# Sliding-window attention and a gated conv FFN on one core: part of the conv in 32x32 tiles, with a new order of the work

## The chip, the cores and the metric

The kernel runs on one core of one Trainium2 chip. The metric is the device time of one execution in microseconds (us); the time before is the median of three runs, 217.72 us (216.22 to 221.8). A core has the engines TensorE (PE, with its weight loads as PEld), VectorE (DVE), ScalarE (ACT), GpSimd (POOL) and SyncE (SP, which issues DMAs here).

## The reference

Batch 8, 8 heads, 576 positions, head width 64; model width 512, hidden width 1024.

```python
scores = scale * np.matmul(q, k.transpose(0, 1, 3, 2))
mask = np.abs(pos[:, None] - pos[None, :]) <= 32
attn = softmax(np.where(mask, scores, -1e9))
x = np.matmul(attn, v).transpose(0, 2, 1, 3).reshape(B, S, 512)

h = np.maximum(x @ w_in, 0.0)
conv_out[:, s] = sum(conv_w[k] * h[:, s + k - 1] for k in range(3))   # per channel, zero outside
gate = 1.0 / (1.0 + np.exp(-conv_out))
out = (h * gate) @ w_out
```

## The kernel before

The program is one long list of steps, `ORDER`. Each word is a step's name with its arguments and, after `@`, the PSUM banks. A loop at the end of the kernel calls the steps in this order, and the class `Pinned` keeps every engine's instructions in program order; semaphores come from the dependences. So each engine, and the DMA queue of SyncE, is a queue in the order of the list, and what waits at its head holds up what is behind it. Nearly all instructions are issued through `Pinned`, which is why the profile shows them all under one line, L189; they are told apart by the tiles' names.

**Attention**, for batch b and half of the heads G: `lq`/`lk` load q and k (576 KB each), `cq`/`ck` cast them to bf16 (the last letter of a step tells the engine: a ScalarE, d VectorE, p GpSimd), `tq`/`tk` turn them on VectorE. `lv` loads a block of v, `cv` casts it into `ve`, `vo` makes a copy of `ve` that is shifted by 64 rows (two copies on an engine, or `t`, two DMAs). `sc` makes the scores of four or five tiles of 64 queries: 32 or 40 products of 32 rows by 128 columns, four at a time. The window's mask comes either from eight more matmuls on TensorE (`m`) or from `mk`, a product after the exponential `ex`. `av` multiplies by v, `nr` divides by the sum. The result is turned either by a DMA transpose (`xt`) or by TensorE (`xp`) and a copy (`xe`).

**FFN.** The 8 x 576 positions are cut into chunks of 384; the first two are halved. That makes 14 pieces P (four halves of 192, ten of 384). The hidden 1024 channels are eight blocks of 128, taken in four pairs m2, so there are 56 pairs. For each pair: `ph` (eight matmuls into PSUM), `re` (relu on ScalarE, into `hT`), `pc` (conv of three taps), `th` (tanh on ScalarE, since the gate is taken as 1 + tanh with the halves folded in), `ga` (gate on VectorE, into `gT`). Then `py` multiplies 128 rows by `w_out` (eight matmuls), `ye` copies from PSUM, `st` stores.

The conv is per channel, so as a matmul its weights are diagonal: `diag_w`, made by `dg`. `pc` has several kinds:

- P: whole 128x128 diagonals, three taps for each of the two blocks, six matmuls. Y: two taps on TensorE, the third by `tp`.
- A and D: 64x64 diagonals, twelve matmuls, of which four may run at once. The second block of the pair comes out with its two halves of 64 channels swapped. In A three tanh calls put that right, in D up to three gate calls. S swaps by DMA (`sw`).
- X: no matmul. ScalarE makes the first tap, VectorE's `tp` adds the other two by four `scalar_tensor_tensor` calls.

A `z` behind the kind says that the tanh goes to SBUF (`z`) and frees the PSUM bank. The heart of A and D is this:

```python
for kk in range(3):
    for i, m in enumerate(ms):
        for lo in (0, 64):
            to = 64 - lo if i else lo
            tensor.matmul(ps[to:to + 64, i, :], diag_w[lo:lo + 64, m, kk, lo:lo + 64],
                          taps(P, m, kk, lo), start=(kk == 0), stop=(kk == 2))
```

Weights: `li`/`ci` load and cast quarters of `w_in`, `lo`/`co` of `w_out`; they are staged in tiles that are not yet in use. `cw` turns the conv weights by one small matmul.

Of the kernel before, what the change touches and what calls it, by code (L numbers as in the profile page):

```python
# [31 lines left out]
lv,0,4 ck,0,0,p dg,3,a li,1 s7 cq,0,0,a dg,2,d li,2 ck,0,1,p dg,7,a tk,0,0 tq,0,0 li,0 cq,0,1,p tk,0,1 sc,0,0,0,m@0+2  # L32
li,3 cv,0,2,a sc,0,0,1,m@4+6 ex,0,0,0,0 lq,1,0 cv,0,0,p tq,0,1 ex,0,0,0,1 ex,0,0,1,1 lk,1,0 cv,0,1,d sc,0,1,0,m@0+2
ex,0,0,1,0 vo,0,0,d ex,0,1,0,1 sc,0,1,1,d@4+6 lq,1,1 cv,0,3,a dg,4,d av,0,0,0@2 lk,1,1 ex,0,1,1,1 cv,0,4,d nr,0,0,0
ex,0,1,1,0 ex,0,1,0,0 mk,0,1,1,d lv,1,2 ci,1,p vo,0,1,a av,0,1,0@0 nr,0,1,0 lv,1,1 ci,2,p xp,0,1@0 xp,0,0@1 xe,0,1,a
av,0,1,1@2 xe,0,0,d av,0,0,1@4 lv,1,0 ci,0,p nr,0,1,1 ph,0,2@0 ph,0,1@1 nr,0,0,1 re,0,2 lo,0 ci,3,p ph,0,0@2 re,0,1
pc,0,2,Pz@0 re,0,0 xp,0,3@1 lk,2,0 cq,1,0,p th,0,2,Pz pc,0,1,A@2 xp,0,2@4 xe,0,3,a ga,0,2,Pz ph,0,3@0 xe,0,2,a
pc,0,0,Pz@1 th,0,1,A lo,3 ck,1,0,p tq,1,0 ph,1,3@4 re,0,3 ga,0,1,A ph,1,0@5 th,0,0,Pz lq,2,0 cq,1,1,p tk,1,0 re,1,3
ph,1,2@6 re,1,0 xp,0,4@4 ga,0,0,Pz ph,1,1@5 re,1,2 lo,2 ck,1,1,p tq,1,1 xe,0,4,a sc,1,0,0,m@6+0 re,1,1 pc,1,2,P@4 lo,1
ex,1,0,0,1 cv,1,2,p tk,1,1 pc,0,3,P@5 ex,1,0,0,0 ph,2,3@0 th,1,2,P lk,2,1 cv,1,1,p th,0,3,P ga,1,2,P sc,1,1,0,d@6+2  # L40
lq,2,1 cv,1,0,a ph,2,2@1 ga,0,3,P ex,1,1,0,1 vo,1,0,d pc,1,3,Pz@4 re,2,3 ex,1,1,0,0 ph,2,1@5 lv,1,4 co,0,d re,2,2
av,1,0,0@6 th,1,3,Pz sc,1,1,1,m@0+2 mk,1,1,0,d re,2,1 pc,2,2,Pz@4 lv,1,3 ck,2,0,a ga,1,3,Pz nr,1,0,0 pc,1,1,Pz@5
th,2,2,Pz tk,2,0 th,1,1,Pz lq,3,0 co,3,p av,1,1,0@6 pc,2,3,P@4 ex,1,1,1,0 pc,1,0,P@5 ex,1,1,1,1 nr,1,1,0 ph,2,0@0
th,2,3,P lk,3,1 cq,2,0,p s6 th,1,0,P ga,1,1,Pz xp,1,0@6 xp,1,1@7 re,2,0 xe,1,0,a sc,1,0,1,m@0+2 lv,2,1 ga,2,3,P
xe,1,1,a pc,2,1,Y@6 ga,1,0,P co,2,a ph,3,3@4 ga,2,2,Pz lq,3,1 co,1,p tq,2,0 pc,2,0,Y@5 ex,1,0,1,1 ph,3,1@7 ex,1,0,1,0
tp,2,1,Y ph,3,2@2 re,3,3 lv,2,0 ck,2,1,p re,3,1 tp,2,0,Y py,0,2@4 th,2,1,Y re,3,2 ga,2,1,Y th,2,0,Y tk,2,1 lk,3,0
cq,2,1,p pc,3,3,Az@6 lk,4,0 pc,3,1,Dz@0 ye,0,2,a ga,2,0,Y cv,1,4,p py,0,1@2 th,3,1,Dz tq,2,1 th,3,3,Az lv,2,2 cv,1,3,p
ga,3,1,Dz vo,1,1,a sc,2,0,0,m@4+0 py,0,0@3 lv,2,3 cq,3,0,p ye,0,1,d ga,3,3,Az ex,2,0,0,1 lq,4,1 av,1,1,1@6 tq,3,0
ck,3,1,a py,1,0@2 st,0,1 cv,2,1,p nr,1,1,1 ex,2,0,0,0 ye,0,0,a av,1,0,1@0 tk,3,1 ye,1,0,a sc,2,0,1,d@4+6 st,0,0
cq,3,1,p ph,3,0@3 ex,2,0,1,0 nr,1,0,1 lv,2,4 pc,3,2,Pz@2 ex,2,0,1,1 re,3,0 sc,2,1,0,d@4+6 tq,3,1 th,3,2,Pz xp,1,2@0  # L50
st,1,0 ck,3,0,p xp,1,3@1 ex,2,1,0,0 xp,1,4@2 ex,2,1,0,1 pc,3,0,Pz@3 xe,1,3,d xe,1,2,a sc,2,1,1,m@4+6 mk,2,1,0,d
xe,1,4,a lk,4,1 tk,3,0 th,3,0,Pz ph,4,0@0 ex,2,1,1,1 lq,4,0 cv,2,2,p ga,3,2,Pz cv,2,0,a ex,2,1,1,0 ph,4,1@2 lv,3,0
ga,3,0,Pz ck,4,0,a mk,2,0,1,d py,1,2@4 re,4,0 tk,4,0 lv,3,2 cq,4,1,p re,4,1 lq,5,0 cv,2,3,a pc,4,0,A@0 tq,4,1 vo,2,0,t
ye,1,2,a ph,4,3@2 th,4,0,A cv,2,4,d lv,3,3 vo,2,1,d pc,4,1,P@4 lv,3,4 re,4,3 ga,4,0,A av,2,0,1@6 th,4,1,P pc,4,3,Az@2
st,0,2 ck,4,1,p nr,2,0,1 ph,4,2@0 th,4,3,Az ga,4,1,P lk,5,0 cq,4,0,p py,1,1@6 tk,4,1 re,4,2 lv,3,1 cv,3,0,p tq,4,0
pc,4,2,Pz@4 lk,5,1 cv,3,2,a ye,1,1,a ga,4,3,Az av,2,1,1@0 th,4,2,Pz sc,3,0,1,d@2+6 st,1,1 cq,5,0,p nr,2,1,1 ex,3,0,1,1
lv,4,0 av,2,1,0@4 ex,3,0,1,0 ga,4,2,Pz xp,2,4@0 xp,2,2@1 xe,2,4,a sc,3,1,1,m@2+6 xt,2,3 cv,3,3,p nr,2,1,0 py,2,0@0
ex,3,1,1,0 xe,2,2,d cv,3,4,a lv,4,2 mk,3,0,1,d ex,3,1,1,1 st,1,2 av,2,0,0@4 vo,3,1,d py,2,1@1 ye,2,0,a lv,4,3 ck,5,0,p
nr,2,0,0 lv,4,4 cv,3,1,a xp,2,0@0 ye,2,1,a xp,2,1@2 vo,3,0,d sc,3,0,0,d@4+6 xe,2,0,a py,2,2@3 xe,2,1,a tq,5,0 lk,6,1
ck,5,1,p ex,3,0,0,0 lk,6,0 ex,3,0,0,1 tk,5,0 sc,4,1,1,m@4+0 lv,4,1 cv,4,0,p ye,2,2,a av,3,1,1@6 mk,3,0,0,d lq,6,0  # L60
ph,5,0@2 ex,4,1,1,0 nr,3,1,1 ex,4,1,1,1 lq,5,1 cv,4,2,p av,3,0,1@4 re,5,0 st,2,1 sc,3,1,0,m@0+6 nr,3,0,1 pc,5,0,Pz@2
ex,3,1,0,0 lv,5,0 cv,4,3,p ex,3,1,0,1 tk,5,1 xt,3,2 cv,4,4,p sc,4,0,1,d@0+4 th,5,0,Pz ph,5,3@6 vo,4,1,d ex,4,0,1,0
# [24 lines left out]
ex,7,1,0,1 pc,10,3,Xz pc,10,2,Az@0 xt,6,0 py,7,0@2 mk,7,1,0,d th,10,0,Xz tp,10,3,Xz ye,6,0,a pc,10,1,Dz@4 th,10,2,Az
st,6,0 py,7,1@3 ye,7,0,d th,10,1,Dz ga,10,2,Az st,7,0 sc,7,0,0,d@6+0 th,10,3,Xz ph,11,3@4 ga,10,1,Dz ex,7,0,0,1
# [16 lines left out]
def kernel(  # L105
# [98 lines left out]
    def unit(b, G):  # L204
        return 2 * b + G
# [574 lines left out]
```

## Time and profile before

| what | value |
|---|---|
| median of 3 runs | 217.72 us |
| profiled execution | 217.15 us, of which the span 215.4 us |
| TensorE busy | 194.5 us (90%), 3113 matmuls |
| VectorE busy | 186.9 us (87%) |
| ScalarE busy | 181.4 us (84%) |
| GpSimd busy | 62.5 us (29%) |
| DMA | 47.58 MB, mean 221 GB/s; share of the 16 engines 75.4% |
| granted TensorE clock | 0.999 |

Busy time is the union of an engine's instructions, and the ends of matmuls are modelled. Rows of the profile read "line, engine, operation, out<-in, shapes, x count | busy us, mean ns of one | idle time before, and what ended it"; rows of a timeline read "start us, duration us, engine, line, operation". The span runs from the first to the last instruction.

### The profile page before, as it was taken

To read this page: it belongs to the slowest core of one execution; us is meant where nothing else is said; L and a number is where in the kernel's file an instruction comes from. 1 tells how busy PE (TensorE), PEld (TensorE's weight loads), DVE (VectorE), ACT (ScalarE), POOL (GpSimd) and SP (SyncE) were. 2 spreads that over 40 slices of the span, in tenths; PEclk is the share of its full clock that TensorE was granted. 3 is DMA by queue.
4 is the path that set the end of the run, shared out by engine and by line. 5 is a ranking of instruction groups with operands and counts; after the bars stand their busy time and mean duration, and the time that the engine had idled before them with its cause. 6 is when DMAs were issued, how large, how long until landed. Compare 5 with 4: busy or idle time off the path is not lost.

```text
span 215.4 us, 7416 instructions
## 1 busy us (share of the span) xinstructions
PE 194.5 (90%) x3113; PEld 116.0 (54%) x3134; DVE 186.9 (87%) x303; ACT 181.4 (84%) x318; POOL 62.5 (29%) x69
## 2 busy tenths in 40 slices
PE   2076998999999879999999999999999999999994
PEld 1055997855755546655445556455553554545443
DVE  5977499989999998998989898989899889999920
ACT  6686599899998767999977779999889898999951
POOL 5636754565323753340336050100300000000000
PEclk9999999999999999999999999999999999999999
DMA  6999999999999999999986569676236205311143
GB/s 222 315 245 394 382 287 401 332 326 337 315 375 264 324 193 348 288 242 306 262 284 186 128 158 246 138 194 185 102 94 109 97 27 158 95 34 49 53 190 146
DMA packets 63253, 47.58 MB, mean 221 GB/s; under 512 B 50012, under 2 KB 52596, under 8 KB 63220
## 3 DMA queue, kind: packets, MB, share of 16 engines
q1 hardware_dynamic: 63184, 47.10, 75.4%
q8 instruction: 24, 0.39, 0.8%
q14 instruction: 9, 0.07, 0.1%
q10 hardware_dynamic: 36, 0.01, 0.1%
HBM read 32.52 MB, written 9.44 MB: 195 GB/s over the span
## 4 chain that ended last, share of the span: by engine, by line
PE 63%; DVE 18%; ACT 5%; SPq 5%; issue 4%; DMA 4%; DVEq 0%
PE PS L189 63%; SPq L189 5%; DVE gT L189 3%; DVE qT L189 3%; DVE xn L189 3%; DVE kT L189 3%; DVE vo L189 3%; DMA vst<-in_v_dram 2%; DMA out_dram<-y 2%; ACT attn L189 2%; DVE attn L189 1%; ACT hT L189 1%; DVE rec L189 1%; ACT xT L189 1%; DVE xT L189 1%
## 5 line engine op out<-in xcount | busy, mean ns | idle before, releaser
L189 PE MATMUL PS<-xT,w_in_sb 128*128 128x385 bf16 (+3 forms) x448 | 70.9, 309 | 0.5 <-ACT z L189 0.4
L189 PE MATMUL PS<-w_out_sb,gT 128*128 128x512 bf16 (+1 forms) x275 | 65.5, 374 | 1.7 <-issue 0.9
L189 PEld LDWEIGHTS <-w_in_sb 128*128 128x128 bf16 x448 | 41.3, 100 | 22.4 <-issue 2.3
L189 DVE SCALAR_TENSOR_TENSOR gT<-z,hT 128x768 bf16<-128x768 f32 (+4 forms) x55 | 45.3, 838 | 5.2 <-ACT z L189 3.8
L189 ACT ACTIVATE hT<-PS 128x770 bf16<-128x770 f32 (+3 forms) x56 | 40.2, 731 | 6.8 <-PE PS L189 6.4
L189 PEld LDWEIGHTS <-gT 128*128 128x128 bf16 x296 | 26.9, 98 | 30.7 <-issue 2.8
L189 ACT ACTIVATE attn<-PS 128x512 bf16<-128x512 f32 (+1 forms) x64 | 39.0, 657 | 3.1 <-PE PS L189 2.7
L189 POOL TENSOR_SCALAR qb<-st 128x1152 bf16<-128x1152 f32 x25 | 32.2, 1288 | 30.7 <-DMA st<-in_q_dram 13.1
L189 ACT ACTIVATE z<-PS 64x384 f32<-64x384 f32 (+4 forms) x66 | 33.6, 512 | 4.4 <-PE PS L189 3.4
L189 DVE SCALAR_TENSOR_TENSOR z<-hT,conv_w_sb,z 128x384 f32<-128x384 bf16 x56 | 31.1, 618 | 0.6 <-ACT z L189 0.6
L189 PE MATMUL PS<-hT,diag_w 64*64 64x384 bf16 (+3 forms) x404 | 27.9, 307 | 0.0
L189 DVE TENSOR_TENSOR xn<-PS,rec 128x512 bf16<-128x512 f32 (+1 forms) x32 | 26.4, 824 | 1.1
L189 ACT COPY y<-PS 128x512 f32<-128x512 f32 (+1 forms) x30 | 17.3, 581 | 9.8 <-PE PS L189 8.9
L189 POOL TENSOR_SCALAR ve<-vst 128x512 bf16<-128x512 f32 x23 | 15.4, 676 | 33.3 <-DMA vst<-in_v_dram 26.0
L189 PE MATMUL PS<-qT,kT 32*128 32x64 bf16 x1152 | 15.7, 195 | 5.3 <-DVE qT L189 5.1
L189 DVE STREAM_TRANSPOSE qT<-qb 128x576 uint32<-128x576 uint32 x16 | 19.9, 1244 | 0.5 <-POOL qb L189 0.3
L189 DVE STREAM_TRANSPOSE kT<-qb 128x576 uint32<-128x576 uint32 x16 | 19.9, 1244 | 0.4 <-ACT qb L189 0.4
L189 PEld LDWEIGHTS <-diag_w 64*64 64x64 bf16 (+1 forms) x404 | 14.5, 104 | 10.4 <-issue 6.8
L189 PEld LDWEIGHTS <-kT 32*128 32x128 bf16 x1152 | 13.5, 96 | 10.8 <-issue 5.1
L189 PEld LDWEIGHTS <-attn 128*64 128x64 bf16 x640 | 13.3, 117 | 9.5 <-issue 6.3
L189 PE MATMUL PS<-ve,attn 128*64 128x65 bf16 x384 | 16.0, 203 | 2.4 <-ACT attn L189 1.4
L189 ACT ACTIVATE z<-hT,conv_w_sb 128x384 f32<-128x384 bf16 x28 | 15.7, 610 | 0.2
(53 smaller groups left out, 158.6 us busy)
## 6 DMA issues: line engine op xcount, KB each, us to landing
st<-in_k_dram SPq DMA_DIRECT2D x16, 576.0 KB, 6.3
st<-in_q_dram SPq DMA_DIRECT2D x16, 576.0 KB, 7.6
out_dram<-y SPq DMA_DIRECT2D x35, 256.0 KB, 2.8
vst<-in_v_dram SPq DMA_DIRECT2D x24, 256.0 KB, 6.1
vst<-in_v_dram SPq DMA_DIRECT2D x16, 192.0 KB, 5.8
vo<-ve SPq DMA_DIRECT2D x16, 130.0 KB, 2.4
xT<-in_moe_w_in_dram SPq DMA_DIRECT2D x2, 512.0 KB, 6.3
xT<-in_moe_w_out_dram SPq DMA_DIRECT2D x2, 512.0 KB, 7.0
```

The lines of the kernel that those rows point to most:

```text
L189: return lambda *args, **kwargs: tc.keep_in_program_order(do(*args, **kwargs))
```

## The change

1. **Conv of four blocks at once** (`pq`, kind Q) for six groups of two pairs, 12 of the 56: piece 5, 7 and 9 for blocks 4 to 7, piece 6, 8 and 11 for blocks 0 to 3. The diagonals are 32x32. Four row groups of four blocks are 16 tiles, each tap 16 matmuls, 48 in all. Block i comes out turned by 32 i channels; so that one tanh and one gate call serve a pair, the input of blocks 1 to 3 is turned beforehand: `rt` copies it by six DMAs into `hR`, and the weights of a Q group are turned likewise.
2. **Conv weights in three parts**: `cw` (matmul), `cwx` (copy to SBUF), and `cx0`, `cx`, `cxx` (a doubled copy, four turned matmuls, and a copy that picks the turned weights). `dg` now makes 64x64 diagonals, `dh` 32x32 ones. Kind P uses 64x64 diagonals too, twelve matmuls on two tiles. Small setup tiles live in two of the `y` tiles.
3. **Kinds S and Y go**, with `sw`.
4. **A new order**, for every engine. The counts of steps whose number changes:

| step | before | after |
|---|---|---|
| `pc` A (full, half) / D (full, half) / S | 16, 2 / 5, 1 / 2 | 7, 0 / 3, 0 / 0 |
| `pc` P (full, half) / Y half | 3, 11 / 2 | 2, 13 / 0 |
| `pc` X (full, half) | 14, 0 | 16, 3 |
| `pq` Q groups, `rt` | 0 | 6 (two pairs each) |
| `sc` with the mask on TensorE / `mk` d / `mk` p | 15 / 15 / 2 | 26 / 3 / 3 |
| `xt` / `xp` with `xe` (a, d) | 22 / 18 (14, 4) | 32 / 8 (7, 1) |
| `vo` DMA / VectorE / ScalarE | 8 / 6 / 2 | 3 / 12 / 1 |
| `cv` a / d / p | 10 / 7 / 23 | 11 / 2 / 27 |
| `cq`, `ck` a / d / p | 6 / 1 / 25 | 6 / 0 / 26 |
| `dg` a / d / p; `dh` d / p | 3 / 4 / 1; none | 1 / 0 / 7; 1 / 1 |

The diff, cut to its core (of the order only two lines with a Q group):

```diff
-lk,0,0 s5 s1 s3,d lq,0,0 s9 lk,0,1 s0,d lq,0,1 s4 lv,0,2 cw@0 lv,0,0 s2 s10 lv,0,1 dg,5,d dg,0,p lv,0,3 dg,6,d dg,1,a
+lq,0,0 s1 s2 s9 s0,d s4 s1d cw@2 lk,0,0 lk,0,1 lv,0,3 cq,0,0,p ck,0,0,a s10 cwx s7 dg,4,p tq,0,0 ck,0,1,p dg,5,a
...
+lv,7,3 ex,7,0,0,1 ex,7,0,0,0 ye,7,1,a ye,7,0,a pc,10,1,Az@0 av,7,0,0@2 av,7,1,0@4 ph,11,2@6 tp,10,0,Xz nr,7,0,0
...
+st,7,1 rt,11,0 xt,7,0 st,6,1 st,6,2 tp,11,2,Xz py,8,0@5 py,8,2@3 sc,7,0,1,d@6+0 py,8,1@2 ex,7,0,1,0 ex,7,0,1,1
+th,11,2,Xz pq,11,0,Qz@0+6 py,7,2@4 mk,7,1,1,d tp,11,3,Xz th,11,3,Xz th,11,1,Qz mk,7,0,1,d ga,11,3,Xz ga,11,2,Xz
...
+    hR_ = tiles(2, [128, 3, CH + 4], BF16, "hR")
-    diag_w = tiles(1, [128, MB, 3, 128], BF16, "diag_w")[0]
+    diag_w = [pp.tile([128, MB // 4, 4, 3, x], BF16, name=f"diag_w{x}") for x in (32, 64)]
...
+    def rt(P, q):
+        c, half = pieces[P]
+        kind = c % 3
+        n = CH + (4 if kind == 1 else 2)
+        h = hT_[kind].rearrange("p (q i) x -> p q i x", i=4)
+        for i in range(1, 4):
+            for p0, p1, a in ((0, 128 - 32 * i, 32 * i), (128 - 32 * i, 128, 0)):
+                sync.dma_start(hR_[q][p0:p1, i - 1, 0:n], h[a:a + p1 - p0, q, i, 0:n])
...
+    def tap(ps, P, m, kk, n, lo, to, h=None, i=0):
+        tensor.matmul(
+            ps[to:to + n], diag_w[n // 64][lo:lo + n, m // 4, m % 4, kk, :],
+            taps(P, m if h is None else i, kk, (lo, n), h), start=(kk == 0), stop=(kk == 2),
+        )
...
-        if kind[0] in "PY":
-            kks = (0, 1, 2) if kind[0] == "P" else (0, 2)
-            for i, m in enumerate(ms):
-                for kk in kks:
-                    tensor.matmul(
-                        ps[:, i, :], diag_w[:, m, kk, :], taps(P, m, kk),
-                        start=(kk == kks[0]), stop=(kk == kks[-1]),
-                    )
+        elif kind[0] == "P":
+            for i, m in enumerate(ms):
+                for kk in range(3):
+                    for lo in (0, 64):
+                        tap(ps[:, i, :], P, m, kk, 64, lo, lo)
...
+    def pq(P, q, kind, banks):
+        w = width(P)
+        for kk in range(3):
+            for i in range(4):
+                for r in range(4):
+                    tap(
+                        PS[:, banks[i // 2] + i % 2, 0:w], P, 4 * q + i, kk, 32, 32 * r, 32 * ((r + i) % 4),
+                        hR_[q] if i else None, i - 1,
+                    )
...
+    def cx(bank):
+        where["cx"] = PS[:, bank, 0:3 * MB]
+        for i in range(4):
+            tensor.matmul(
+                PS[:, bank, 3 * MB * i:3 * MB * i + 3 * MB], conv_w24[:, 32 * i:32 * i + 128], ident24,
+                start=True, stop=True,
+            )
...
+    def dh(q, e):
+        to = diag_w[0][:, q].rearrange("p i k x -> p (i k) x")
+        {"d": vector, "p": gpsimd}[e].tensor_tensor(
+            out=to, in0=eye32[:, None, :].broadcast_to([128, 12, 32]),
+            in1=conv_w_sb[0][:, q].rearrange("p i k -> p (i k)")[:, :, None].broadcast_to([128, 12, 32]),
+            op=ALU.mult,
+        )
```

More of the change, by code (lines that the diff above doesn't have):

```diff
@@ L36 @@
[L36 to L50, printed above, removed]
@@ L167 @@
     unit_ = band[:, 256:384].rearrange("p (e x) -> p e x", e=2)
-    band2 = tiles(1, [128, 192], BF16, "band2_")[0]
-    mask1 = tiles(1, [128, 64], BF16, "mask1_")[0]
-    conv_w24 = tiles(1, [3 * MB, 128], FP32, "conv_w24")[0]
+    once = y_[NY - 2]
+    mask1, eye32 = once[:, 0:32].bitcast(BF16), once[:, 32:48].bitcast(BF16)
+    eye64 = once[:, 128:160].bitcast(BF16)
+    conv_w_sb = [
+        t.rearrange("p (q i k) -> p q i k", i=4, k=3)
+        for t in (once[:, 48:48 + 3 * MB], tiles(1, [128, 3 * MB], FP32, "conv_w_sb")[0])
+    ]
+    conv_w24, ident24 = y_[NY - 1][0:3 * MB, 0:256], y_[NY - 1][0:3 * MB, 256:256 + 3 * MB]
     PS = pq.tile([128, 8, 512], FP32, name="PS")
@@ L207, in slot @@
     def slot(y, b, G):
[L208 to L211 removed]
+        return 4 * b + 2 * G + y
     def load_qk(y, b, G, *s_e):
[L216 to L224 removed]
         *s, e = s_e or ("s",)
@@ L241, in cast_qk @@
         cols = slice(s[0] * n, s[0] * n + n) if s else slice(0, 2 * n)
-        if b >= LATE:
-            cols = slice(0, 512 * len(blocks(G)))
         i = slot(y, b, G)
@@ L465, in re, with taps @@
         scalar.activation(to, ps, AF.Relu, bias=0.0, scale=0.5)
-    def taps(P, m, kk, part=None):
+    def taps(P, m, kk, part=None, h=None):
         c, half = pieces[P]
@@ L533, in pc, with tap_w @@
                     for lo in (0, 64):
-                        to = 64 - lo if i else lo
-                        tensor.matmul(
-                            ps[to:to + 64, i, :], diag_w[lo:lo + 64, m, kk, lo:lo + 64],
-                            taps(P, m, kk, lo), start=(kk == 0), stop=(kk == 2),
-                        )
+                        tap(ps[:, i, :], P, m, kk, 64, lo, 64 - lo if i else lo)
+    def pq(P, q, kind, banks):
+        w = width(P)
+        for kk in range(3):
[5 more added lines that the diff above has]
+                    )
+        for y in range(2):
+            m2 = 2 * q + y
+            where["pc", P, m2] = psum2(banks[y], w, True)
+            if kind[1:] == "z":
+                z_of(P, m2)
+    def tap_w(m, kk):
+        return conv_w_sb[1][:, m // 4, m % 4, kk:kk + 1]
     def tp(P, m2, kind):
-        ps = where["pc", P, m2]
-        for kk in ((1,) if kind[0] == "Y" else (1, 2)):
+        for kk in (1, 2):
             for i in range(2):
                 m = 2 * m2 + i
-                o = like(ps[:, i, :], P)
+                o = like(where["pc", P, m2][:, i, :], P)
                 vector.scalar_tensor_tensor(
-                    out=o, in0=taps(P, m, kk), scalar=conv_w_sb[:, kk, m:m + 1], in1=o,
-                    op0=ALU.mult, op1=ALU.add,
+                    out=o, in0=taps(P, m, kk), scalar=tap_w(m, kk), in1=o, op0=ALU.mult, op1=ALU.add
                 )
@@ L556, in tanh @@
             scalar.activation(out_, in_, AF.Tanh, bias=0.0, scale=1.0)
-        if kind[0] == "S":
-            tanh(where["z0s", P, m2], ps)
-            return
         if kind[0] != "A":
@@ L639, in cw @@
     def cw(bank):
-        tensor.matmul(PS[:, bank, 0:3 * MB], conv_w24, ident24, start=True, stop=True)
-        vector.tensor_copy(out=conv_w_sb.rearrange("p k m -> p (k m)"), in_=PS[:, bank, 0:3 * MB])
-    def dg(m, e):
-        if e != "a":
-            {"d": vector, "p": gpsimd}[e].tensor_tensor(
-                out=diag_w[:, m, :, :], in0=ident[:, None, :].broadcast_to([128, 3, 128]),
-                in1=conv_w_sb[:, :, m:m + 1].broadcast_to([128, 3, 128]), op=ALU.mult,
-            )
-        else:
-            for kk in range(3):
-                scalar.activation(
-                    diag_w[:, m, kk, :], ident, AF.Copy, bias=0.0, scale=conv_w_sb[:, kk, m:m + 1]
-                )
+        where["cw"] = ps = PS[:, bank, 0:3 * MB]
@@ new lines, in cw, with cwx, cx0 @@
+        tensor.matmul(ps, conv_w24[:, 0:128], ident24, start=True, stop=True)
+    def cwx():
+        vector.tensor_copy(
+            out=conv_w_sb[1].rearrange("p q i k -> p (q i) k"), in_=where["cw"].rearrange("p (k m) -> p m k", k=3)
+        )
+    def cx0():
+        vector.tensor_copy(out=conv_w24[:, 128:256], in_=conv_w24[:, 0:128])
+    def cx(bank):
[5 more added lines that the diff above has]
+            )
@@ new lines, in cxx @@
+    def cxx():
+        ps = where["cx"]
+        vector.tensor_copy(
+            out=conv_w_sb[0].rearrange("p q i k -> p i q k"),
+            in_=bass.AP(ps.tensor, ps.offset, [list(ps.ap[0]), [3 * MB + 1, 4], [4, MB // 4], [MB, 3]]),
+        )
+    def dg(m, e):
+        to, w = diag_w[1][:, m // 4, m % 4], conv_w_sb[1][:, m // 4, m % 4]
+        if e == "a":
+            for kk in range(3):
+                scalar.activation(to[:, kk, :], eye64, AF.Copy, bias=0.0, scale=w[:, kk:kk + 1])
+            return
+        {"d": vector, "p": gpsimd}[e].tensor_tensor(
+            out=to, in0=eye64[:, None, :].broadcast_to([128, 3, 64]),
+            in1=w[:, :, None].broadcast_to([128, 3, 64]), op=ALU.mult,
+        )
```

236 lines of the change are left out of this document (96 added, 140 removed).

## The prediction

> **What bounds the kernel now.** I read the page first (engine totals, then the 40 slices), then busy time by window, then TensorE's timeline, the groups by shape, and the tile view of `vo`.
>
> ```profile
> PE 194.5 (90%) x3113; PEld 116.0 (54%) x3134; DVE 186.9 (87%) x303; ACT 181.4 (84%) x318; POOL 62.5 (29%) x69
> ...
> PE   2076998999999879999999999999999999999994
> ...
> DVE  5977499989999998998989898989899889999920
> ACT  6686599899998767999977779999889898999951
> ...
> DMA  6999999999999999999986569676236205311143
> ```
>
> TensorE works in nine tenths or more of nearly every slice after the start, VectorE almost as much. The start is DMA: the queue is full, TensorE is not. The windows put numbers on that:
>
> ```profile
> 0.00:30.00 30.00, 17.51 (x358) 15.16 (x358) 22.30 (x52) 21.13 (x42) 18.64 (x27) 1.00 0.95 305
> 30.00:200.00 170.00, 164.60 (x2675) 94.78 (x2694) 158.62 (x244) 151.91 (x263) 43.89 (x42) 1.00 0.77 214
> 200.00:215.40 15.40, 12.42 (x83) 6.01 (x82) 6.00 (x10) 8.33 (x15) 0.00 (x0) 0.99 0.36 136
> ```
>
> Columns are length, then busy us of PE, PEld, DVE, ACT, POOL, then clock, DMA share, GB/s. From 30 to 200 us TensorE is busy 97%, VectorE 93%, ScalarE 89%. TensorE bounds, VectorE is four points behind, so a saving on TensorE alone is soon VectorE's time. The granted clock is 1.00 throughout and plays no part.
>
> Busy time overstates TensorE where matmuls overlap, so I price a step of the order from its first matmul to the next step's first:
>
> ```profile
> 130.21 0.40 PE L189 MATMUL PS<-band 32*128 32x256 bf16 x8
> 130.44 0.41 PE L189 MATMUL PS<-qT,kT 32*128 32x64 bf16 x32
> 130.78 1.48 PE L189 MATMUL PS<-xT,w_in_sb 128*128 128x385 bf16 x8
> ...
> 135.96 0.68 PE L189 MATMUL PS<-hT,diag_w 64*64 64x384 bf16 x12
> 136.57 1.90 PE L189 MATMUL PS<-w_out_sb,gT 128*128 128x512 bf16 x8
> 138.41 0.68 PE L189 MATMUL PS<-hT,diag_w 64*64 64x384 bf16 x12
> 139.02 0.42 PE L189 MATMUL PS<-qT,kT 32*128 32x64 bf16 x32
> ```
>
> A four-tile conv pair costs 0.61 us (136.57 - 135.96), the eight mask matmuls of a score step 0.23, its 32 products 0.34. In the same way: whole-array conv pair 1.07 (half piece 0.52), `ph` 1.34, `py` 1.83, `xp` 0.27. All steps together make 190.9 us. Of these 12.9 were begun by 30 us; the other 178.0 took the remaining 185.4, so 7.4 us are lost after the start, 2.9 of them the last copy and store.
>
> **The change, TensorE.** *Conv before:* 23 four-tile pairs x 0.615 + 3 halves x 0.35 + 3 whole-array x 1.07 + 11 halves x 0.52 + 2 two-tap halves x 0.34 = 24.8 us; the 14 X pairs cost TensorE nothing. *After:* 10 x 0.615 + 2 x 1.07 + 13 x 0.52 = 15.1 us, 19 X pairs, and six Q groups of two pairs, 48 matmuls of 32x32 each. No Q is in the trace. From below, three rounds in which sixteen tiles run at once: a whole-array stream is 1.07/6 = 0.179 us, so 0.54. From above, four tiles at a time: 12 x 0.179 = 2.15. The nearest row is the four-tile pair, whose three rounds take 0.615; issuing is no limit, since 40 score products go in 0.42 us (10.5 ns each; 48 make 0.50). I take 0.65, six make 3.9. Conv: 19.0 - 24.8 = -5.8.
>
> *Matmul floor, by a page:* the Trainium skill, "TensorE: Matmul & The Clock Gate", section "Wait — 56ns, not 53.3ns?", says matmul starts are never closer than about 25 ns. By it, as an estimate, a Q group would be 48 x 25 = 1.2 us and the six 3.3 us dearer. The 10.5 ns between score products here contradict it, so I leave it out.
>
> *Masks and transposes:* 26 instead of 15 score steps get the mask from TensorE (+11 x 0.25 = +2.7), and 8 instead of 18 blocks are turned by `xp` (-10 x 0.27 = -2.7). The `cx` matmuls fall in the start, where TensorE waits for inputs; without that cover they would cost some 0.6. Net: **-5.8**, leaving 185.1 besides `cx`, 185.7 with it.
>
> **VectorE and ScalarE.**
>
> ```profile
> L189 DVE SCALAR_TENSOR_TENSOR z<-hT,conv_w_sb,z 128x384 f32<-128x384 bf16 x56 | 31.1, 618 | 0.6 <-ACT z L189 0.6
> ...
> L189 ACT ACTIVATE z<-PS 64x384 f32<-64x384 f32 x32 | 15.5, 485 | 0.6
> ```
>
> ```profile
> L189 SPq DMA_DIRECT2D vo<-ve x16: 462/574/2524, 61.9 to 147.6; - x16
> L189 DVE COPY vo<-ve x12: 424/426/1385, 13.5 to 88.5; 64x1040 bf16<-64x1040 bf16 x12
> ```
>
> The figures after the first colon of the tile view are min/median/max ns. VectorE: `vo` 12 steps instead of 6, +8.1 at the mean of the old ones (two copies of 0.675); `tp` on 2 more full and 3 half pairs less 2 two-tap ones, +7.6; `mk` 3 for 15, -8.9; gates, one call of 0.95 where a crossed pair needs up to three, -3.1; `xe` -2.1; casts -2.1 (`cv`) and -1.1 (`ck`); `dg` -2.2 (to GpSimd, half as wide); small things +0.8. Sum -3.0, or -2.9 busy: 184.0. The soft number is `vo`: its copy takes 424 ns alone and up to 1385 while GpSimd works, so 24 copies cost 10 to 33 us; I take 16.2; GpSimd's extra 12 us of work (seven `dg`, one `dh`, four `cv`, a `mk`) could make it dearer.
>
> ScalarE: crossed four-tile tanh needs 0.497 + 2 x 0.485, a Q pair one call of 0.81; 18 crossed pairs become 7, -7.2. `xe` -3.5, `vo` -2.1, `dg` -2.0, X taps +4.5, `cv` +0.6: -9.7, some -8.9 busy. No bound.
>
> **Queues and start.** SyncE gains 36 copies for `rt` and 10 transposes and loses ten `vo` and four `z` copies. A `vo` copy is 0.574 us of issue, a transpose 1.25 (two in 2.52 us):
>
> ```profile
> 117.54 2.52 SPq L189 DMA_TRANSPOSE xT<-xn  x2
> 120.16 1.17 SPq L189 DMA_DIRECT2D vo<-ve  x2
> ```
>
> That is 20.9 + 12.5 - 8.3 = +25 us of SyncE time, most of it between `py` 2 and `py` 7. `pq` is a new wait: relu (0.8) -> six copies issued (3.5) -> landing (1.8, what `vo` shows after its issue) = 6.1 us. Hiding it is TensorE work between the last `ph` of the group and its `pq`: counted from the order, about 7.7 us at the tightest (piece 11), 8 to 12 elsewhere. Without cover the whole 6.1 is paid, with scores and `py` queued behind `pq`, and ScalarE's exp behind those. A transpose or two ahead in the queue (1.25 each) uses up the slack; I book 1.0 for all six.
>
> In the start two more loads of 576 KB stand ahead of the `w_in` quarters. GpSimd's `w_in` casts began at 17.36, 18.74, 20.07 and 21.45, 1.36 us per 512 KB, so the first quarter comes 3.1 us later, near 20.5, the last near 27.6. The first scores come earlier, one load being moved behind them. Stepping through the new order by hand to `sc 1 1 0` I get 13.0 us of TensorE steps by 30 us against 12.9. I count nothing (bounds -1 and +2).
>
> **Sum.** TensorE: 30 + (185.7 - 13.0) + 7.4 = 210.1. VectorE: 184.0, less 22.3 in the start and 1.1 of last copies, is 160.6; at 93% of the time, 172; so its last gate ends at 202.1. Half a us on, `py` 11 in four parts (5.5) and the 2.9 at the end give 211.0. I take 210.3 between the two and 1.0 for the `pq` waits: a span of 211.3. The profiled execution has 217.15 for a span of 215.4, so 1.75 outside: **213.0 us**. That execution lies 0.6 below the median 217.72, so against the median it is -2.2%, close to the 2% that a measurement of this kernel can just tell.
>
> **Rivals.**
>
> *A copy port that stays free* (209 or less). If the 12 `vo` steps meet an idle GpSimd, VectorE sheds 6 us more, is out of the way, and the loss after the start shrinks by 3: 215.4 - 5.8 - 3 + 1.75 = 208.4. For: half of the old copies took 424 to 427 ns. Against: GpSimd has 12 us more to do.
>
> *Q runs four tiles at a time* (222). Then +1.5 x 6 = 9. For: four row groups write one block, at different partitions of one bank. Against: the four-tile pair does that with two row groups, and 0.615 is far below the 6 x 0.179 = 1.07 of two at a time. The Trainium skill, "TensorEngine Tiling (Array Packing)", section "Restrictions and Gotchas", holds that different row tiles can't use one bank at once; by that rule Q would be this rival, and the trace speaks against it.
>
> *SyncE late* (224, slower). One mechanism: the `rt` copies stand behind transposes, loads and stores in one queue, and these wait for their own producers. If each of six groups reaches TensorE 2 us late, 12 us join the 211.9 of the bare TensorE line. It decides as soon as SyncE reaches `rt` more than 1.6 us after the relu in the tightest group. For: about 56 us of issue in a stretch with 63 of TensorE work. Against: the DMA share is down to a half by then, so copies land quickly.
>
> *The new order holds less well* (218). It is a wholly new order. At 94% after the start instead of 96, the gain is given back: 2% of 173 is 3.5, and 1.5 more from the start.
>
> **How the numbers follow.** Forecast 0.42, free port 0.16, four at a time 0.07, SyncE late 0.22, order 0.13. The forecast's own range is 210 to 216.5; the 2% line (213.4) cuts it, 0.29 below and 0.13 above. Faster: 0.29 + 0.16 = 0.45. Same: 0.13 + 0.05 of Q + 0.09 of the order = 0.27. Slower: 0.22 + 0.02 + 0.04 = 0.28. The range takes in the free port with Q at 0.54 (206.5) and SyncE late with a little over (225).
>
> **What would show it.** `hT`,`diag_w` groups of 32x32 with about 0.65 us to the next step (over 1 us: Q wrong); TensorE waits on DMA into `hR` under 2 us in all (over 8: SyncE late); VectorE near 184 busy with `vo` copies averaging 0.68; 13 us of TensorE steps by 30 us. A span above 215 with Q at 0.65 and no `hR` waits would make the sum wrong in its loss term, under 208 in its VectorE term.

## The result and the profile after

The changed kernel takes 225.03 us (median of 4 runs, 222.89 to 226.02), the kernel before, in the same comparison, 218.45 (216.22 to 221.8). The ratio is 1.037, 95% interval [1.030, 1.043]: slower, where 213.0 was forecast. The profiled execution of after is 224.56 us with a span of 222.8. Single runs of one kernel lie up to 5 us from its median. Some runs of a kernel, whatever it is, are slowed down by some per cent, so the ratios are taken from the other runs alone (the medians from all), and `a_noq_d` and `a_st_pool`, with only one of these in four, have none.

The totals and slices of the page of after:

```profile
PE 198.0 (89%) x3351; PEld 118.5 (53%) x3374; DVE 184.0 (83%) x299; ACT 171.3 (77%) x292; POOL 73.6 (33%) x91
...
PE   1478999896998988887999999989999999999994
...
DVE  4887988989569986981699989997999998899930
ACT  2895799875958936784778889689859988898941
...
PEclk9999999999999999996799999999999999999999
DMA  6999997997989999957999869986866554242043
```

VectorE and ScalarE have less to do than before (184.0 for 186.9, 171.3 for 181.4), and TensorE's 198.0 for 194.5 are partly at a lower clock. But slices 8 to 19 of TensorE have sixes, sevens and eights, VectorE and ScalarE have holes there, and in two slices the granted clock falls to 0.6 and 0.7. The windows (columns as in the prediction) say where the time went:

```profile
0.00:30.00 30.00, 20.29 (x429) 16.80 (x430) 23.91 (x50) 19.93 (x37) 23.26 (x43) 1.00 0.98 310
30.00:200.00 170.00, 158.09 (x2795) 91.87 (x2814) 146.43 (x228) 136.83 (x232) 50.36 (x49) 0.98 0.86 217
200.00:222.80 22.80, 19.59 (x132) 9.88 (x132) 13.67 (x23) 14.52 (x25) 0.00 (x0) 1.00 0.31 116
```

Between 30 and 200 us TensorE is busy 93% instead of 97%, VectorE 86% instead of 93%. No engine's work became the bound; all wait more. I priced TensorE's steps as in the prediction and took the sum of the steps begun by a time from that time. The loss is 16.2 us at 30 us (before 17.1), 23.1 at 90 (20.6), 30.1 at 110 (20.1), 33.4 at 150 (21.1), and then stays. So about ten of the twelve lost us go between 90 and 150 us.

The first Q group stands there. TensorE's timeline (in brackets the idle time before an entry and what ended it):

```profile
95.68 2.98 PE L195 MATMUL PS<-xT,w_in_sb 128*128 128x386 bf16 x17
99.39 0.34 PE L195 MATMUL PS<-hT,diag_w 32*32 32x384 bf16 x4 [0.74 <-ACT hT L195]
99.79 0.73 PE L195 MATMUL PS<-hR,diag_w 32*32 32x384 bf16 x6
100.78 0.34 PE L195 MATMUL PS<-hR,diag_w 32*32 32x384 bf16 x2 [0.26 <-DMA hR<-hT]
101.29 0.32 PE L195 MATMUL PS<-hR,diag_w 32*32 32x384 bf16 x1 [0.18 <-DMA hR<-hT]
102.10 0.50 PE L195 MATMUL PS<-hR,diag_w 32*32 32x384 bf16 x3 [0.49 <-DMA hR<-hT]
...
103.17 0.61 PE L195 MATMUL PS<-band 32*128 32x256 bf16 x8
103.57 0.64 PE L195 MATMUL PS<-qT,kT 32*128 32x64 bf16 x32
```

The group comes in drops, one copy into `hR` after the other, and takes 103.17 - 99.39 = 3.78 us. The piece 8 group takes 2.55. The others take 0.74 to 0.97, so Q itself is not far from the 0.65 that was forecast. After it the same score step that took 0.42 us takes 0.64. The windows of 2 us around this place show why:

```profile
100.00:102.00 2.00, 1.17 (x9) 0.30 (x6) 0.00 (x0) 0.05 (x1) 0.94 (x1) 0.91 0.38 81
102.00:104.00 2.00, 1.90 (x75) 1.20 (x74) 0.10 (x1) 0.81 (x1) 0.00 (x0) 0.50 0.83 244
104.00:106.00 2.00, 1.30 (x49) 1.02 (x41) 0.97 (x2) 1.74 (x3) 0.00 (x0) 0.50 1.06 241
106.00:108.00 2.00, 2.00 (x45) 1.16 (x38) 1.95 (x3) 1.26 (x4) 0.60 (x1) 0.50 1.03 396
108.00:110.00 2.00, 2.00 (x47) 1.28 (x46) 0.46 (x2) 1.82 (x3) 1.62 (x2) 0.89 1.08 332
```

The clock stands at 0.50 from about 101.6 to 108.4 us: 3.4 us of TensorE time at most. VectorE and ScalarE do next to nothing from 100 to 104, as what they work on comes from TensorE.

And the queue of SyncE ahead of that group, where relu (`re`) had ended at 90.38:

```profile
87.23 3.79 SPq L195 DMA_TRANSPOSE xT<-xn  x1
91.08 0.57 SPq L195 DMA_DIRECT2D out_dram<-y  x1
91.75 3.41 SPq L195 DMA_TRANSPOSE xT<-xn  x2
95.25 0.52 SPq L195 DMA_DIRECT2D st<-in_k_dram  x1
95.88 4.15 SPq L195 DMA_DIRECT2D hR<-hT  x5
```

SyncE reaches `rt` at 95.88, 5.5 us after the relu. In the other groups it is 5.3, 4.6, 2.8, 0.5 and 0.4 us late. Adding up the queue's rows from 90 to 150 us, SyncE spends 52.2 of 60 us issuing (before 44.9) and has gaps of over 0.2 us for 3.1 us in all (before 11.5): in that stretch it has hardly any room.

### The profile page after: what moved, and what is told of

Read it like the earlier page. It is cut to its first block, busy times and chain, and to the rows that moved or that the text cites. A ratio compares the mean times of both kernels' runs of the same rounds, so it can differ in the third digit from the quotient of the medians.

```text
span 222.8 us, 7903 instructions
## 1 busy us (share of the span) xinstructions
PE 198.0 (89%) x3351; PEld 118.5 (53%) x3374; DVE 184.0 (83%) x299; ACT 171.3 (77%) x292; POOL 73.6 (33%) x91
## 4 chain that ended last, share of the span: by engine, by line
PE 60%; DMA 17%; SPq 7%; ACT 5%; DVE 4%; issue 3%; POOL 2%; POOLq 0%; DVEq 0%; ACTq 0%
PE PS L195 60%; DMA st<-in_k_dram 7%; SPq L195 7%; DMA xT<-xn 3%; DMA hR<-hT 3%; ACT attn L195 2%; DMA vst<-in_v_dram 2%; DMA out_dram<-y 2%; POOL attn L195 1%; DVE kT L195 1%; ACT z L195 1%; POOL qb L195 1%; DVE xn L195 1%; DVE y L195 1%; ACT y L195 1%
## 5 line engine op out<-in xcount | busy, mean ns | idle before, releaser
L195 PE MATMUL PS<-w_out_sb,gT 128*128 128x512 bf16 (+1 forms) x273 | 64.5, 373 | 1.9 <-issue 1.0
L195 DVE SCALAR_TENSOR_TENSOR gT<-z,hT 128x768 bf16<-128x768 f32 (+2 forms) x56 | 46.0, 846 | 9.5 <-ACT z L195 8.9
L195 ACT ACTIVATE hT<-PS 128x770 bf16<-128x770 f32 (+3 forms) x56 | 39.6, 728 | 9.6 <-PE PS L195 9.1
L195 DVE SCALAR_TENSOR_TENSOR z<-hT,conv_w_sb,z 128x384 f32<-128x384 bf16 (+1 forms) x76 | 42.5, 626 | 0.2
L195 ACT ACTIVATE z<-PS 128x768 f32<-128x768 f32 (+2 forms) x43 | 26.1, 621 | 7.0 <-PE PS L195 6.7
L195 POOL TENSOR_SCALAR ve<-vst 128x512 bf16<-128x512 f32 x27 | 18.7, 704 | 22.9 <-DMA vst<-in_v_dram 22.8
L195 PE MATMUL PS<-hT,diag_w 64*64 64x192 bf16 (+2 forms) x372 | 21.8, 297 | 0.8 <-ACT hT L195 0.7
L195 ACT ACTIVATE z<-hT,conv_w_sb 128x384 f32<-128x384 bf16 (+1 forms) x38 | 20.3, 591 | 0.2
L195 PE MATMUL PS<-band 32*128 32x256 bf16 (+1 forms) x208 | 14.0, 309 | 5.7 <-ACT band L195 4.2
L195 PEld LDWEIGHTS <-kT 32*128 32x128 bf16 x1152 | 15.3, 97 | 6.0 <-issue 4.3
```

The costliest lines, as they stand in the source:

```text
L195: return lambda *args, **kwargs: tc.keep_in_program_order(do(*args, **kwargs))
```

## The experiments

Each ratio is to the kernel before, run beside it on the same chip, with its 95% interval. Kernels named `a_` start from after, `b_` from before.

**Is it the order, the Q groups, the queue's loads, or TensorE's transposes?**

`b_order`: the new code with the old order.

```diff
-ORDER: after's
+ORDER: before's, its two S pairs as A, its two Y halves as P; no rt, no pq
```

> The changed program with the old order: the conv weights are made the new way (64x64 diagonals, cw and cwx), no Q group, two S pairs made A, two Y halves made P. If the loss lies in the new order of work (theory O), this runs like before: 217 to 220 us. If the new way of the weights and the P kind on two tiles cost something by themselves, 222 or more.

Measured 222.18 us, 1.018 [1.006, 1.029]. So even the old order loses some 2% with the new code.

`a_noq`: the six groups as two A pairs each.

```diff
-rt,5,1  ...  pq,5,1,Qz@0+4  th,5,2,Qz  ga,5,2,Qz
+             pc,5,2,Az@0 pc,5,3,Az@4  th,5,2,Az  ga,5,2,Az
```

> The changed kernel with the six Q groups undone: each is two A pairs at the same place, and the 36 rt copies are gone. Theory Q (the rt copies and the waits of pq hold the kernel up): pq took 6.3 us over its price in the trace, two A pairs cost TensorE 0.4 us more each; with SyncE 21 us freer 217 to 220 us. Theory S (early transposes in SyncE's queue hold the loads up, between 40 and 110 us): only the waits at 99, 146 us go, 221 to 224 us. Theory O: 223 to 226.

Measured 225.19 (221.35 to 227.48), 1.024 [1.008, 1.039]. Without Q and its copies nothing is won. By its ranges that spoke for theory O, but it could not tell: the A pairs that take Q's place cost about as much as the copies (see `a_nort` and `a_noq_d`).

`a_xp12`: seven of the DMA transposes go back to TensorE.

```diff
-xt,1,3
+xp,1,3@4 xe,1,3,a        (and 1,4 1,2 2,0 2,1 2,2 2,4)
```

> The changed kernel with the seven DMA transposes of batches 1 and 2 made by TensorE again (xp and xe on ScalarE, at the same place of the order). Theory S: DMA no longer runs dry at 49 to 56 and 64 to 66 us, the loss between 30 and 110 us falls from 13.9 by half or more; TensorE pays 1.9: 217 to 221 us. Theory Q: 224 to 227 us (the price of xp on top).

Measured 229.94, 1.049 [1.033, 1.066]. Theory S fell, and the time is over the range of theory Q too: 9 us off SyncE's queue in the early part bought nothing.

`a_loads`: within each cluster of SyncE's steps, `rt` first, then loads, then transposes and stores.

```diff
-xt,2,0 xt,2,1 ... lv,4,0 lv,4,2
+lv,4,0 lv,4,2 lq,5,0 lk,5,0 xt,2,0 xt,2,1
```

> The changed kernel with the order of SyncE's queue alone changed: within each run of DMA steps that stand together in the order, the rt copies come first, then the loads, then transposes, stores and vo. Theory S: 219 to 222 us, since loads no longer wait behind transposes that wait for xn. Theory Q: 222 to 224 by the earlier rt alone. Theory O: no change, 224 to 226.

Measured 240.4, 1.105 [1.095, 1.114], over all three ranges. The loads had not been what was late for TensorE; the stores and transposes put behind them are. The waits of this kernel (engine, line, what it waited for, us in all, times, longest) show it:

```profile
ACT y L195 <- DMA out_dram<-y: 23.7, 6, 7.9
...
PE PS L195 <- ACT y L195: 12.2, 4, 6.4
...
PE PS L195 <- DMA xT<-xn: 4.3, 2, 3.9
```

A tile `y` is free for the next `ye` only when its store has landed. ScalarE waits for that in its `ye`, and TensorE waits for ScalarE; this is more than what TensorE waits for the transposes themselves.

**Is it the copies?**

`a_nort`: no copies; `hR` is set to zero once, so three of four blocks in a Q group see zeros.

```diff
-rt,5,1   (and the five others)
+        for t in hR_:
+            gpsimd.memset(t, 0.0)
```

> The changed kernel with the rt copies left out; the turned input of the Q groups is zeros written once, so three of four blocks of a group get no conv. TensorE's 48 matmuls a group stay. Theory SyncE late (SyncE reached rt 5.5, 5.3, 4.6, 2.8, 0.5 and 0.4 us after the relu, and pq waited): the waits go and SyncE has 21 us less to issue, 216 to 219 us. Theory DMA traffic (transposes and loads are late by themselves): 222 to 224.

Measured 215.05 (213.57 to 218.17), 0.992 [0.975, 1.009]. Its profile:

```profile
30.00:200.00 170.00, 163.30 (x2890) 95.82 (x2902) 154.91 (x247) 147.14 (x248) 51.91 (x52) 1.00 0.84 212
200.00:212.10 12.10, 8.69 (x47) 4.51 (x48) 2.94 (x5) 4.19 (x9) 0.00 (x0) 1.00 0.40 152
```

TensorE is back at 96%, the clock at 1.00, and the span is 212.1 where the forecast had 211.3. With Q's matmuls kept, leaving the copies out takes away the whole loss against before, as far as the interval can tell.

**Can they stand elsewhere?** `a_rt_act` issues them from ScalarE's queue, `a_rt_pool` from GpSimd's, `a_rt_early` leaves them with SyncE but right behind the group's second relu.

```diff
-                sync.dma_start(hR_[q][p0:p1, i - 1, 0:n], h[a:a + p1 - p0, q, i, 0:n])
+                scalar.dma_start(hR_[q][p0:p1, i - 1, 0:n], h[a:a + p1 - p0, q, i, 0:n])
```

> The changed kernel with the 36 rt copies issued from ScalarE's queue, behind the relu that makes their input, instead of SyncE's. Theory SyncE late: the copies start at once, 219 to 222 us, the rest of the gain being lost to some 20 us of issue on ScalarE, which was busy 171 of 223. If what costs is the copies' landing, no change: 223 to 226.

> The changed kernel with the rt copies issued from GpSimd's queue, which was busy 74 us of 223. Theory wait: the copies start when the relu ends unless a cast or a load's wait stands ahead of them in GpSimd's queue; 217 to 222. Theory issue: SyncE is rid of 21 us, 216 to 220. If GpSimd's own waits for loads hold the copies up: over 225.

> The changed kernel with each rt moved forward in SyncE's queue to right behind the second relu of its group, ahead of the transposes, stores and loads that stood before it. Theory SyncE late by its order: pq no longer waits, 220 to 223 us. Theory SyncE late by its sum (it has too much to issue between 85 and 150 us, whatever the order): the transposes come later instead, 224 to 229.

ScalarE: 243.51, 1.122 [1.103, 1.141]. GpSimd: 224.74, 1.024 [1.014, 1.034]. SyncE early: 231.25, 1.060 [1.038, 1.082]. On ScalarE's timeline:

```profile
91.98 8.54 ACTq L195 DMA_DIRECT2D hR<-hT  x6
100.57 0.70 ACT L195 ACTIVATE attn<-PS 128x640 bf16<-128x640 f32 x1 [10.95 <-DMA hR<-hT]
```

Six issues there keep ScalarE from its exp and relu for 8.5 us, and TensorE stands still behind it. On GpSimd the copies wait for the relu with casts behind them (the tile view of `hR` has its idle time ahead of them and what ended it):

```profile
L195 POOL DMA_DIRECT2D hR<-hT x36: 501/517/740, 89.1 to 184.3; - x36
its engine sat idle before it (us, times) until:
  ACT hT L195: 22.3, 6
```

Early on SyncE, `rt` is issued within 1 us of the relu, and the time is worse: now the transposes and stores come later. The longest wait of TensorE, from 127 to 134 us, is again for a `ye`, which waits for a store:

```profile
133.38 0.59 ACT L195 COPY y<-PS 128x512 f32<-128x512 f32 x1 [7.47 <-DMA out_dram<-y]
...
134.01 3.26 PE L195 MATMUL PS<-w_out_sb,gT 128*128 128x512 bf16 x8 [6.75 <-ACT y L195]
```

In none of the three other places are the copies free.

**The waits or the issuing?** `a_rt_nowait` issues all 36 copies, but the Q groups read `hT` unturned and wait for none.

```diff
-                        hR_[q] if i else None, i - 1,
+                        None, i - 1,
```

> The changed kernel with all 36 rt copies issued, but pq reads hT as it stands instead of the turned hR, so three of four blocks of a group get other channels' input. SyncE has the same to issue, TensorE no longer waits for a copy. Theory wait (what costs is pq, first in TensorE's queue, waiting for the landing): 215 to 218 us, as without the copies (215.05). Theory issue (21 us of issue hold up the transposes, loads and stores behind them): 221 to 225.

Measured 222.5, 1.017 [1.012, 1.022]. Against 1.037 the waits are worth 2.0% (4.3 us); against 0.992, 36 copies that nobody waits for still cost 2.5% (5.5 us). With intervals of 1 to 2% on both differences, neither part can be called the larger. A piece of the second part is the wait seen above: TensorE waits 3.0 us for a `ye` (in `a_rt_one` 0.3).

```profile
ACT y L195 <- DMA out_dram<-y: 9.9, 4, 5.2
...
PE PS L195 <- ACT y L195: 3.0, 3, 1.9
```

`a_rt_one` makes one unturned copy of a group's six; `a_rt_tiny` makes all six, but of 16 columns each. The first edit is that of `a_rt_tiny`; the line of the second stands in `a_rt_one` in place of `rt`'s two loops.

```diff
-                sync.dma_start(hR_[q][p0:p1, i - 1, 0:n], h[a:a + p1 - p0, q, i, 0:n])
+                sync.dma_start(hR_[q][p0:p1, i - 1, 0:16], h[a:a + p1 - p0, q, i, 0:16])
```
```diff
+        sync.dma_start(hR_[q][:, :, 0:n], h[:, q, 1:4, 0:n])
```

> The kernel after, but each group's six copies into hR are one copy of the same bytes. It is not turned, so three of the four blocks get the input of other channels. Issuing falls from 36 copies to 6, about 16 us less on SyncE; bytes and packets stay. Theory I (what costs is SyncE's time for issuing, and what is queued behind it): 217 to 219, ratio 0.995 to 1.005, and the group's wait is shorter by five issues. Rival T (what costs is the copies' own traffic and their landing): 223 to 226, as after. Between the two, 220 to 222: both.

> The kernel after, but each of the 36 copies moves only the first 16 columns of its rows (32 bytes instead of 772 or 776); the rest of hR is zero from the start, so three blocks of a Q group see mostly zeros. Issuing and the waits stay, the bytes go (1.8 MB). Theory I (issuing): 223 to 226, as after. Rival T (traffic): 217 to 220.

One copy: 216.53, 0.994 [0.988, 1.001]. Six small ones: 222.83, 1.023 [1.017, 1.030]. The intervals are apart. The tile view of `hR` has the durations (min/median/max ns) of after, of one copy, and of the small ones:

```profile
L195 SPq DMA_DIRECT2D hR<-hT x36: 497/549/1609, 95.9 to 185.1; - x36
```
```profile
L195 SPq DMA_DIRECT2D hR<-hT x6: 489/650/1530, 93.3 to 171.9; - x6
```
```profile
L195 SPq DMA_DIRECT2D hR<-hT x36: 496/548/1839, 94.0 to 182.8; - x36
```

An issue takes 0.55 us (median) whether it moves 32 bytes a row or 772, and 0.65 for the bytes of all six copies at once. So 30 issues less are some 18 us of SyncE's issuing (165.2 us in all in after, 147.4 with one copy) and 4.2% of the kernel's time; a twenty-fourth of the bytes is worth 1.3%, with intervals that touch. SyncE's gaps between 90 and 150 us go the same way: 3.1 us in after, 3.9 with small copies and 2.1 in `a_rt_nowait`, against 7.9 with one copy and 7.6 without any. The cost is the number of issues in a queue with hardly any room (fewer of them also shorten a group's own wait), and only to the smaller part the bytes.

`a_q2` keeps Q only in pieces 9 and 11, where SyncE was on time; the four others are A pairs as in `a_noq`.

> The changed kernel with the four Q groups undone that SyncE served late (pieces 5, 6, 7, 8, by A pairs), the two of pieces 9 and 11 kept, whose copies began 0.5 and 0.4 us after the relu. If a late copy costs and a Q group is worth 1 to 2 us of TensorE and ScalarE by itself: 219 to 223, better than both six groups (225.0) and none (225.2). If the order only suits six groups, 225 or more.

Measured 222.51, 1.015 [1.006, 1.024]: a part of the loss is gone. `a_st_pool` takes the 37 stores of the output from SyncE to GpSimd:

```diff
-        sync.dma_start(out_rows[r0:r0 + 128, part(x)], y_[(3 * c + i) % NY][:, part(x)])
+        gpsimd.dma_start(out_rows[r0:r0 + 128, part(x)], y_[(3 * c + i) % NY][:, part(x)])
```

> The changed kernel with the 37 output stores issued from GpSimd's queue instead of SyncE's, where they stood 0.33 to 2 us each and waited for ye. Theory issue: SyncE gets to rt and the transposes earlier, 218 to 222. Theory wait with late landing only: 222 to 225. If GpSimd, now waiting for ye in its queue, is late with its casts: over 226.

Median 227.9, so no gain showed; without a ratio it says no more.

**Is a part of it the clock?** `a_fill5` gives TensorE twelve matmuls in the wait of piece 5, `a_fill11` the same in piece 11, where it hardly waits.

```diff
+        for _ in range(12 if P == 5 else 0):
+            tensor.matmul(
+                PS[:, banks[0], 0:w], w_in_sb[:, 0, 0:128], w_in_sb[:, 0, 0:w], start=True, stop=True
+            )
```

> The kernel after, with twelve whole-array matmuls of 384 columns (w_in by itself, results overwritten by the conv) put ahead of the Q group of piece 5, where TensorE waits 3 us for hR and the granted clock then stands at 0.50 for about 7 us, 3.4 us lost. At 0.179 us each they fill 2.1 us of that wait. Theory C (part of the loss is the halved clock behind the stall): the clock stays at 1.00 and the time falls by 2 to 3.5, to 221.5 to 223. Rival (the clock's fall is hidden by what TensorE waits for there anyway): 225 to 226, as after, whatever the clock does. If the filler itself only delays: 226 to 227.

> The kernel after, with the same twelve matmuls ahead of the Q group of piece 11, which waits for hR only some 0.2 us: a control. They should cost what they take, less that wait: 226.5 to 227.5, with the clock's mean as after (0.985). If it is 225 or less, TensorE had time to spare there too.

Piece 5: 1.023 [1.010, 1.036], from three runs at 222.1 to 223.7 us, clock 0.998 to 1.0; the median over all six is 225.04. Piece 11: 226.18, 1.035 [1.027, 1.044]. In the profiled run of `a_fill5` the clock is 1.00 from 95 to 115 us, in that of `a_fill11` 0.66 from 100 to 105, so the filler does hold it at piece 5. But the intervals overlap, and the runs behind the ratio of `a_fill11` take 223.9, 225.4 and 226.6 us at a clock of 0.998 to 1.0, and 225.8 and 226.5 at 0.992 and 0.985. That the halved clock adds time is not shown; 3.4 us is its ceiling in the profiled run of after.

**What is Q worth, and how touchy is an order?** `a_noq_d` has two D pairs for each group instead of `a_noq`'s A pairs.

> The kernel after without Q and its copies: each of the six groups becomes two D pairs (twelve 64x64 matmuls, one tanh call, up to three gate calls on VectorE). With two A pairs instead (three tanh calls on ScalarE) it was 225.2 against 215.05 for Q without copies, 10 us for 3.5 us more of TensorE steps. If ScalarE's extra calls make that up, D gives 218 to 221; if TensorE's time does, or what comes behind it in the order, D gives 224 to 227; VectorE's own extra calls (about 24 x 0.3 us = 7 us) could bring it there as well, then VectorE would be near 190 us busy.

Its profiled run is 224.08, with VectorE 193.4 us busy. So it is not ScalarE's calls alone: on VectorE they cost about as much, in one run. Between the profiled spans of `a_noq` (219.6) and `a_nort` (212.1) lie some 2.3 us of TensorE steps (twelve A pairs at 0.615 against 5.1 for the six Q groups of `a_nort`) and 5 us of loss; what each call adds to that loss stays open.

`b_p64` gives the kernel before the two 64x64 tiles of kind P; `b_dup2` gives it one matmul more in each of its 13 half pairs on whole diagonals. Both add some 1.1 us of TensorE steps.

```diff
+                    for lo in (0, 64):
+                        tensor.matmul(
+                            ps[lo:lo + 64, i, :], diag_w[lo:lo + 64, m, kk, lo:lo + 64], taps(P, m, kk, lo), ...
```
```diff
+                if i == 0 and w < CH:
+                    tensor.matmul(ps[:, i, :], diag_w[:, m, 0, :], taps(P, m, 0), start=True, stop=True)
```

> The kernel before with one part of the change: whole-array conv pairs (P) and the two-tap ones (Y) on two 64x64 tiles, twelve or eight matmuls instead of six or four. The changed kernel's trace has 0.59 against 0.51 us for a half pair and 1.13 against 1.07 for a full one: 16 pairs, 1.2 us, so 219 to 221 us, 0.5% slower. If the old order with the new weights lost 1.8% by these pairs, 1% or more shows here; if by its other parts or by chance, nothing.

> The kernel before, with one matmul more in each of its 13 half-piece conv steps on whole diagonals (the first tap is done once more ahead, as a group of its own): 13 x 0.09 = 1.1 us more of TensorE steps, no wait more and no other change; the output stays the same. With two 64x64 tiles in these steps, 1.2 us more of TensorE, the kernel before took 2.3% longer [1.0%, 3.6%]. If an order with TensorE at 97% passes such work on one to one: 218.5 to 220, ratio 1.003 to 1.008. If the order is so tight that every us shifts other queues into one another: 221 to 224, ratio 1.015 or more.

`b_p64`: 222.01, 1.023 [1.010, 1.036]. `b_dup2`: 216.07, 0.990 [0.984, 0.996]. Both theories on `b_dup2` fell: more work, and not slower. In its profile the 12 `vo` copies on VectorE are at their short time:

```profile
L189 DVE COPY vo<-ve 64x1040 bf16<-64x1040 bf16 x12 | 5.1, 426 | 0.9 <-ACT ve L189 0.4 <-issue 0.2
```

That is 3.0 us less than the 8.1 of before, and the likely reason, though one profile does not show it. A small change can shift such an order by 1 to 2% either way, by a mechanism that no run here shows; so the 2% of `b_order` and `b_p64` can't be put down to the two tiles with certainty. No kernel with the whole computation beat the one before by 2%.

## Why the prediction was wrong

**The step that failed** is "I book 1.0 for all six", with the +25 us of SyncE's time behind it, which I put beside other work. The copies cost about 10 us (225.03 against 215.05). Three things in that step were wrong:

- *The chain.* I worked out relu, 3.5 us of issuing, 1.8 of landing: 6.1 us against a cover of 7.7 to 12. The chain of piece 5 is 5.5 us until SyncE comes, 4.8 of issuing, and 1.4 until the last landing at 102.06: 11.7 in all. "A transpose or two ahead in the queue (1.25 each)" were two transposes of 3.4, a store and a load, behind a third transpose that began before the relu was done and took 3.79. From the start of an issue to its landing the median in after is 4.0 us, where 0.57 and 1.8 were counted.
- *What else is late.* I priced the wait of TensorE for `hR`, not what stands behind `rt` in SyncE's queue. That is about half: 2.5% with no wait for a copy at all (`a_rt_nowait`), in part by stores and loads that came late.
- *The sum of the queue.* My own figure, 56 us of issuing in 63 of TensorE work, stood in a rival's "for". I had treated these issues as hidden work. Measured, SyncE issues for 52.2 of 60 us with 3.1 of gaps, and they were not hidden.

The rival *SyncE late* (224) is what happened, by its time and mostly by its mechanism: SyncE was more than its 1.6 us late in four of six groups, though not in piece 11, which I had counted as the tightest (0.4). But it took each group to be 2 us late at TensorE, 12 us in all, so its 224 is in part luck. The six groups lost 5 us in their own steps (9.8 against 5.1 in `a_nort`); the rest came by way of the queue and perhaps the clock. And the sign that I gave for it, over 8 us of TensorE waiting for `hR`, did not come: the tile view has 1.4 us. A Q group that comes in drops shows mostly as matmuls, and hardly as idle time; the time to the next step shows it.

**Points that held.** The two bounds gave a span of 210.3 without the 1.0 for the copies; with the copies left out it is 212.1, and the small terms below would make up the 1.8 between. Even so, the ratio of `a_nort`, 0.992 [0.975, 1.009], does not tell the forecast gain from none. VectorE was forecast at 184.0 busy and has 184.0, but by luck, as errors cancel: `vo` takes 12.1 us (503 ns each) where I took 16.2; the X taps rose by 9.8 us (32.7 to 42.5, with the two-tap ones) where 7.6 were booked; and some 2 us more are spread over small steps.

```profile
L195 DVE SCALAR_TENSOR_TENSOR z<-hT,conv_w_sb,z 128x384 f32<-128x384 bf16 (+1 forms) x76 | 42.5, 626 | 0.2
...
L195 DVE COPY vo<-ve 64x1040 bf16<-64x1040 bf16 x24 | 12.1, 503 | 2.2 <-POOL ve L195 1.6
```

ScalarE's -8.9 busy was -10.1. By 30 us, 13.8 us of steps had begun against 13.0. "7.4 us are lost after the start", 4.5 of them ahead of the last copy and store, nearly holds without the copies (5 to 7 us between 30 and 190 us in `a_nort`) and fails with them (17 to 18).

**Small terms.** A Q group takes 0.74 us and more, not 0.65; the half P pair on two tiles 0.59, not 0.52: together 1.8 us too little. Forty-eight matmuls in 0.74 us are 15 ns apart, so the floor of 25 ns of the Trainium skill, "TensorE: Matmul & The Clock Gate", section "Wait — 56ns, not 53.3ns?", was rightly left out. The same 0.74 us rules out the rival of Q running four tiles at a time (222), which needs 2.15. The rule beside that rival, of the Trainium skill, "TensorEngine Tiling (Array Packing)", section "Restrictions and Gotchas", that different row tiles can't use one bank at once, is not what these tiles show: four row groups write one bank, each at other partitions. Two figures do not come out of the prediction's own terms: 206.5 (208.4 less 0.7 for Q at 0.54 is 207.7), and -2.2%, which sets a profiled time against a median; against the profiled 217.15, 213.0 is -1.9%.

**What I had not in the sum at all**: "The granted clock is 1.00 throughout and plays no part". In after it is 0.985 to 0.992 in every run. In all four runs of `a_nort` and three of four of `a_rt_one` it is 1.0. `a_rt_nowait` has both, so the wait at piece 5 is not its only cause. What it cost is not shown.

## What to carry to other kernels

Add up each DMA queue's issue time, and its gaps, over the stretch where the new DMAs go, as for an engine. Here, with gaps of 3 us left of 60, 36 copies of 0.55 us or more cost 10 us, half of it by what stood behind them; and in three other places, an earlier one or another engine's queue, they cost as much or more. Count issues before bytes, and look for a layout that needs one copy where six are written. Judge a wait by the time from a step to the next one, since a step fed in drops is counted as busy.

## What was unexpected of the hardware

- The issue of a copy on SyncE takes 0.55 us for 16 columns and for 386; on ScalarE's queue six take 8.5 us, in which ScalarE does nothing else. One DMA transpose took 3.79 us to issue, where the median is 1.24.
- The clock granted to TensorE fell to 0.50 for 6.8 us though TensorE was counted busy for 1.17 of 2 us just before, and its longest full stop was 0.74 us. The Trainium skill, "TensorE: Matmul & The Clock Gate", section "Why this matters for your kernels", asks for no idle gaps over about 3 us between bursts. The trace agrees with the half rate, but not with the gap: it fell here behind 3 us of a trickle of 32x32 matmuls, and stayed at 1.00 in `a_fill5`, where twelve whole-array matmuls filled that stretch.
